# A statically scheduled spectral and attention kernel: background matmul jobs cut into pieces, VectorE operations placed around GpSimd, new scheduler constants

## Chip, cores, metric

One core of one Trainium2 chip. The metric is device time in microseconds (us) of one execution. Before: 1383.79 us, median of 3 runs (1383.43 to 1384.35). Engines: PE is TensorE (PEld its weight loads), DVE is VectorE, ACT is ScalarE, POOL is GpSimd.

## The reference

Two pairs of layers over a sequence of 2048 rows of 512: an FFT filter with a residual, then attention with 32 query heads and one shared K and V of 16 channels (the code is abbreviated here).

```python
def _A_ref(x, w_r, w_i):                     # spectral filter
    X = rfft2(x.astype(float32)) * (w_r + 1j * w_i)
    return irfft2(X).astype(bfloat16)
def _B_ref(x, wq, wk, wv, wo):               # 32 heads of 16, one K and V
    q, k, v = heads(x @ wq), x @ wk, x @ wv
    p = softmax(einsum("bhqd,bkd->bhqk", q, k) * 16 ** -0.5)
    return merge(einsum("bhqk,bkd->bhqd", p, v)) @ wo
x = x + _A_ref(_layernorm(x), A_w_r, A_w_i)
x = x + _B_ref(_layernorm(x), B_wq, B_wk, B_wv, B_wo)
# ... and both once more
```

## The kernel before

The program is written by a list scheduler in Python. It keeps a clock for each engine, chooses the next instruction by it, and emits every engine's stream in that order. On the chip the streams run in order and meet at semaphores. The order is fixed, so an engine that is late makes the others wait.

Softmax tiles are shared out. ACT exponentiates pairs (`exp`); DVE makes single tiles by an affine map to the bits of a bfloat16 (`p1`), and POOL adds two constant offsets to those bits (`phase`). PE makes scores, 32-row matmuls, and the products with V ("pv"), 32-column matmuls. Everything else on PE is a *background job* of full 128x128 matmuls, put between scores and pv. Each of these three tile shapes is a *mode* of PE; background jobs are the *full* mode.

```python
class Plan:
    MM, ACT_EXP, DVE_P1, POOL_PH = 216.0, 905.0, 600.0, 1200.0     # (cut: more constants)
    WARM, FORCE, HOLD, GAP = 3500.0, 3150.0, 200.0, 3000.0         # (one line each in the kernel)
    def do_bg(self, start, k):                # a background job goes in whole
        eng = k.eng
        if eng == "PE":
            self.fill(start, "full")          # filler matmuls where PE was too idle
            # (cut)
        k.fn(k)
        k.end = self.t[eng] = start + k.dur
    def pe_next(self):
        # (cut: candidates for scores and pv)
        c += self.bg_next("PE")
        return self.least(c)

# a projection: four matmuls, 870 ns, one job
m = p.add("PE", 870.0, deps, lambda k, r=r: em.proj(at, t, r, k.slot, 0, 4), take="b", prio=-2, gap=p.GAP)

def phase(self, t, p, n, eng):
    if eng == "POOL":
        self.nc.gpsimd.int64_add(t[p][:, 0:n].bitcast(U64), t[0][:, 0:n].bitcast(U64), DELTA[p] * FOUR)
    # (cut)
def mul(self, at, b):                         # normalise: two inputs in SBUF, on DVE
    # (cut)
    self.nc.vector.tensor_tensor(out=on.rearrange("p a h d -> p h a d"), in0=raw[:, :, :, 0:16],
                                 in1=rc.unsqueeze(3).to_broadcast([P, 2, 16, 16]), op=ALU.mult)
```

The FFT butterflies (`radix4`) are DVE operations with two SBUF inputs too. Some of those for layer 2 run within layer 1's attention. `fill` adds matmuls on zeros when the last 3.4 us of PE's plan hold too little work.

The softmax here doesn't subtract the row's maximum and nothing guards it: scores larger than these inputs give would overflow.

## Time and profile before

| stretch (us from the start) | what | us |
|---|---|---|
| 0 to 125.3 | FFT; then K and V are built, with first scores | 125.3 |
| 125.3 to 702.0 | attention 1, from DVE's first tile to its last | 576.7 |
| 702.0 to 812.9 | FFT and build of layer 2 | 110.9 |
| 812.9 to 1370.2 | attention 2 | 557.3 |
| 1370.2 to 1381.0 | last projections | 10.8 |

The borders are the first and last bit-trick tile of DVE in each layer. From the page of the kernel before: busy time by engine, two lines of the busy tenths (the span in 40 slices, each digit the busy share of one in tenths), and three groups of instructions (busy us, mean ns, idle before them and what ended it).

```profile
PE 1333.4 (97%) x13112; PEld 439.6 (32%) x13112; DVE 1309.3 (95%) x2345; ACT 1249.1 (90%) x1396; POOL 828.6 (60%) x805
...
DVE  6987999999999999999979879999999999999998
ACT  6488999999999999999954889999999999999996
...
L1085 ACT ACTIVATE e<-sa 128x1024 bf16<-128x1024 f32 x1251 | 1175.1, 1037 | 46.1 <-PE sa L1080 27.1
L1096 POOL INT64_ADD w<-w x795 | 826.2, 1051 | 541.9 <-DVE w L1092 494.0
L1092 DVE TENSOR_SCALAR w<-b 128x512 uint16<-128x512 f32 x1594 | 984.3, 681 | 15.6 <-PE b L1080 8.9
```

DVE and ACT are nearly full in attention and less so in two short stretches. A busy time includes the overlap with the next instruction: exponentials start every 904 ns and DVE tiles every 598 ns when nothing holds them up. The same by stretch (busy us of each engine, granted clock, DMA):

```profile
core 0: us, PE busy (x) PEld busy (x) DVE busy (x) ACT busy (x) POOL busy (x), PEclk, DMA share, GB/s
0.00:125.30 125.30, 119.04 (x884) 63.34 (x885) 99.94 (x263) 85.40 (x123) 2.35 (x10) 1.00 0.29 90
125.30:702.00 576.70, 561.37 (x5730) 161.99 (x5730) 566.12 (x948) 555.33 (x603) 411.46 (x394) 1.00 0.02 5
702.00:812.90 110.90, 105.82 (x810) 56.41 (x810) 89.46 (x223) 67.30 (x94) 1.04 (x1) 1.00 0.15 47
812.90:1370.20 557.30, 541.01 (x5645) 155.81 (x5645) 547.32 (x904) 540.68 (x580) 412.81 (x400) 1.00 0.01 4
```

L1120 is the multiply `mul`, L75 a butterfly step. The view of one line's instructions gives minimum, median and maximum in ns:

```profile
L1120 DVE TENSOR_TENSOR on<-raw,rc x32: 681/686/1539, 150.1 to 1373.6; 128x512 bf16<-128x512 f32 x32
...
L75 DVE TENSOR_TENSOR gx<-w x8: 281/286/1119, 17.3 to 720.6; 128x256 bf16<-128x256 bf16 x8
```

Same operation, same size, yet up to 858 ns longer. The timeline of DVE and POOL around the longest multiply (start us, length us) shows when:

```profile
1056.48 2.01 DVE L1092 TENSOR_SCALAR w<-b 128x512 uint16<-128x512 f32 x3
1058.41 1.54 DVE L1120 TENSOR_TENSOR on<-raw,rc 128x512 bf16<-128x512 f32 x1
1059.87 2.47 DVE L1092 TENSOR_SCALAR w<-b 128x512 uint16<-128x512 f32 x4
...
1057.35 2.06 POOL L1096 INT64_ADD w<-w  x2 [0.52 <-DVE w L1092]
```

POOL's second add begins at 1058.36, 45 ns before the multiply, and ends at 1059.40; the multiply ends half a microsecond later.

### The profile page before, as it was taken

The page shows a single profiled execution, that of the slowest core. Times are in us where ns is not written, and L with a number is a line of the kernel's source. Part 1 is how long each engine was busy: PE and PEld are TensorE (multiplying, and loading weights), DVE is VectorE, ACT ScalarE, POOL GpSimd, SP SyncE. Part 2 cuts the span into 40 slices and gives each one's busy share as a digit, 9 for nine tenths or more (in the row PEclk, how much of TensorE's full clock was granted, in tenths as well). Part 3 has the DMA queues.
Part 4 walks back from the last instruction along what each step waited for, and adds up shares of the span by engine and source line. Part 5 has one row for each costly group of instructions (what it writes and reads, how often), then busy time and mean ns, then how long its engine had stood idle before and what let it go on. Part 6 is the DMA issues. An engine that isn't in the chain of part 4 may idle for free. (4 is left out here: it accounts for less than half of the span.)

```text
span 1381.0 us, 32833 instructions
## 1 busy us (share of the span) xinstructions
PE 1333.4 (97%) x13112; PEld 439.6 (32%) x13112; DVE 1309.3 (95%) x2345; ACT 1249.1 (90%) x1396; POOL 828.6 (60%) x805
## 2 busy tenths in 40 slices
PE   9999999999999999999999999999999999999998
PEld 5643222222223222322246432222222222222222
DVE  6987999999999999999979879999999999999998
ACT  6488999999999999999954889999999999999996
POOL 0001777767775677667730027777777767776775
PEclk9999999999999999999999999999999999999999
DMA  9100000000000000000051000000000000000000
GB/s 284 39 1 1 2 2 2 2 1 2 1 1 2 1 1 2 1 1 1 2 161 39 1 1 2 1 2 13 6 1 2 5 13 2 2 2 17 2 2 16
DMA packets 20937, 22.08 MB, mean 16 GB/s; under 512 B 2096, under 2 KB 19504, under 8 KB 20784
## 3 DMA queue, kind: packets, MB, share of 16 engines
q1 hardware_dynamic: 20496, 19.44, 4.5%
q8 instruction: 102, 1.67, 0.5%
q10 hardware_dynamic: 288, 0.56, 0.1%
q14 instruction: 51, 0.42, 0.1%
HBM read 17.89 MB, written 2.10 MB: 14 GB/s over the span
## 5 line engine op out<-in xcount | busy, mean ns | idle before, releaser
L1085 ACT ACTIVATE e<-sa 128x1024 bf16<-128x1024 f32 x1251 | 1175.1, 1037 | 46.1 <-PE sa L1080 27.1
L1096 POOL INT64_ADD w<-w x795 | 826.2, 1051 | 541.9 <-DVE w L1092 494.0
L1092 DVE TENSOR_SCALAR w<-b 128x512 uint16<-128x512 f32 x1594 | 984.3, 681 | 15.6 <-PE b L1080 8.9
L1102 PE MATMUL b<-w,vs 128*32 128x512 bf16 x4782 | 532.9, 385 | 2.0 <-DVE w L1098 1.3
L1102 PE MATMUL b<-e,vs 128*32 128x512 bf16 x2502 | 434.4, 385 | 1.6 <-ACT e L1085 1.0
L1080 PE MATMUL sa<-w,KB 32*128 32x512 bf16 x1258 | 250.6, 381 | 13.8 <-ACT e L1085 11.0
L1102 PEld LDWEIGHTS <-vs 128*32 128x32 bf16 x7284 | 151.5, 94 | 349.4 <-issue 326.2
L1080 PE MATMUL sa<-w,KA 32*128 32x512 bf16 x1244 | 248.8, 382 | 10.6 <-ACT e L1085 8.0
L1080 PE MATMUL b<-w,KA 32*128 32x512 bf16 x804 | 245.7, 382 | 0.4
L1080 PE MATMUL b<-w,KB 32*128 32x512 bf16 x790 | 241.5, 382 | 2.9 <-DVE w L1092 2.6
L1080 PEld LDWEIGHTS <-KB 32*128 32x128 bf16 x2048 | 82.1, 91 | 234.8 <-issue 229.7
L1080 PEld LDWEIGHTS <-KA 32*128 32x128 bf16 x2048 | 80.4, 91 | 228.2 <-issue 224.2
L1011 DVE TENSOR_TENSOR x_sb<-b,x_sb 128x512 bf16<-128x512 f32 x64 | 42.6, 679 | 11.9 <-PE b L1006 6.0
L1109 DVE STREAM_TRANSPOSE raw<-b 128x512 f32<-128x512 f32 x64 | 45.3, 708 | 1.7 <-PE b L1102 1.6
L846 DVE BATCH_NORM_STATS2 st<-x_sb 128x6 f32<-128x512 bf16 x64 | 43.5, 679 | 3.4 <-DMA x_sb<-in_A_x_dram 3.1
L1064 PE MATMUL b<-gx,wq 128*128 128x512 bf16 x128 | 33.0, 380 | 1.3 <-DVE w L1092 1.0
L1133 PE MATMUL b<-WO,w 128*128 128x512 bf16 x128 | 32.2, 380 | 0.7 <-DVE w L1092 0.2
L987 PE MATMUL b<-it,xd 128*128 128x256 bf16 x256 | 30.0, 273 | 2.5 <-DVE xd L57 2.5
L1006 PE MATMUL b<-tab_PS,w 128*128 128x512 bf16 x128 | 31.4, 381 | 0.0
L896 PE MATMUL b<-tab_PH,e 128*128 128x512 bf16 x128 | 30.8, 380 | 0.6 <-DVE w L1092 0.2
L833 PE MATMUL b<-zero 128*128 128x512 bf16 x76 | 24.1, 411 | 5.3 <-DVE w L1092 2.4
L993 ACT CAST e<-b 128x512 bf16<-128x512 f32 x32 | 18.0, 583 | 12.0 <-PE b L987 12.0
(85 smaller groups left out, 605.2 us busy)
## 6 DMA issues: line engine op xcount, KB each, us to landing
it<-const_IT SPq DMA_DIRECT2D x8, 640.0 KB, 6.4
w<-const_FT SPq DMA_DIRECT2D x8, 512.0 KB, 7.4
x_sb<-in_A_x_dram SPq DMA_DIRECT2D x4, 512.0 KB, 6.8
w<-in_A_w_r_dram SPq DMA_DIRECT2D x8, 256.0 KB, 7.0
w<-in_A_w_i_dram SPq DMA_DIRECT2D x8, 256.0 KB, 7.6
out_dram<-x_sb SPq DMA_DIRECT2D x16, 128.0 KB, 1.8
tab_PH<-const_PH ACTq DMA_DIRECT2D x1, 512.0 KB, 5.0
tab_PS<-const_PS SPq DMA_DIRECT2D x1, 512.0 KB, 7.8
```

Of the source, the lines that this page charges most:

```text
L846: self.nc.vector.bn_stats(st, self.x[:, x[1], x[0], :])
L896: self.nc.tensor.matmul(self.ps(slot), lhsT=xt[:, i, cc, :], rhs=self.PH[:, cc, :], start=(cc == 0), stop=(cc == NC - 1), skip_group_check ...
L1006: self.nc.tensor.matmul(self.ps(slot), lhsT=L.UT[t][:, b, r, 128 * i:128 * i + 128], rhs=self.PS[:, 2 * i + b, :], start=(i == 0 and b == ...
L1011: self.nc.vector.tensor_tensor(out=x, in0=self.ps(slot), in1=x, op=ALU.add)
L1064: self.nc.tensor.matmul(self.ps(slot), lhsT=self.wq[:, c, g * 128:(g + 1) * 128], rhs=self.xTc(at, qb, c), start=(c == 0), stop=(c == NC - ...
L1080: self.nc.tensor.matmul(o, lhsT=KX[rs, kc * P:(kc + 1) * P], rhs=at.QT[qb][rs, g, :], start=True, stop=True, skip_group_check=True)
L1085: self.nc.scalar.activation(out=e, in_=self.ps(slot), func=ACT.Exp, scale=SCALE)
L1092: self.nc.vector.tensor_scalar(out=t[0][:, j], in0=self.ps(slot), scalar1=P1_SCALE, scalar2=P1_BIAS, op0=ALU.mult, op1=ALU.add)
L1096: self.nc.gpsimd.int64_add(t[p][:, 0:n].bitcast(U64), t[0][:, 0:n].bitcast(U64), DELTA[p] * FOUR)
L1102: self.nc.tensor.matmul(self.ps(slot)[32 * h:32 * h + 32, :], lhsT=V[:, kc, :], rhs=rhs, start=first, stop=last, skip_group_check=True)
L1109: self.nc.vector.transpose(out=at.raw[(qb, g)][:, par].rearrange("p a b -> p (a b)"), in_=self.ps(slot))
L1133: self.nc.tensor.matmul(self.ps(slot), lhsT=at.OT[t][:, g, r * P:(r + 1) * P], rhs=self.WO[:, g, :], start=(g == 0), stop=(g == 3), skip_g ...
```

## The change

The intent is to stop a four-matmul background job from holding up a score that is due, and to keep two-input DVE operations out of POOL's way. Arithmetic stays the same. The core of the diff (the same `parts=` is given to nearly every kind of background job, whose emitters now emit one piece):

```diff
-    WARM = 3500.0
-    FORCE = 3150.0
+    WARM = 3600.0
+    FORCE = 3350.0
-    HOLD = 200.0
+    HOLD = 250.0
-    GAP = 3000.0
+    GAP = 0.0
+    SLIP = 250.0
+    PATIENT = 1500.0
+    URGE = 300.0
+    STARVED = 6000.0
@@ bg_next
+            if k.port:
+                busy = self.t["POOL"]
+                for e in self.pool:
+                    if e[0] < max(start, busy) + k.dur:
+                        busy = max(busy, e[0]) + self.POOL_PH
+                start = max(start, busy - 160.0)
             # (cut)
+            if k.step:
+                prio = -4
+            elif eng == "PE" and self.t[eng] - max(ready, k.born) > self.STARVED:
+                prio = -3
@@ do_bg
+            n = min(steps, k.parts - k.step)
+            # (cut) emits n pieces; the job ends with its last piece
@@ pe_next
-        c += self.bg_next("PE")
+        for b in self.bg_next("PE"):
+            k, n = b[3], 99
+            late = T - max(b[4], k.born)
+            if kinds and c[0][0] <= b[0] + k.dur + self.PE_SW:
+                room = max(limit, c[0][0]) + self.SLIP - b[0] - self.PE_SW
+                fit = int(room / (k.dur / k.parts)) if room > 0 else 0
+                left = k.parts - k.step
+                if fit < left:
+                    need = min(left, 2) if late < self.PATIENT else 1
+                    n = max(fit, 1) if late > self.STARVED else fit if fit >= need else 0
+            if n:
+                c.append((b[0] - (self.URGE if kinds and late > self.PATIENT else 0.0),) + b[1:5] + (n,))
@@ jobs
-            m = p.add("PE", 870.0, deps, lambda k, r=r: em.proj(at, t, r, k.slot, 0, 4), take="b", prio=-2, gap=p.GAP)
+            m = p.add("PE", 870.0, deps, lambda k, s, r=r: em.proj(at, t, r, k.slot, s, s + 1), parts=4, take="b", prio=-2, gap=p.GAP)
-        mu = p.add("DVE", 660.0, [rc], lambda k: em.mul(self, b), lazy=tail)
+        mu = p.add("DVE", 660.0, [rc], lambda k: em.mul(self, b), lazy=tail, port=True)
```

The `port` rule also covers the butterflies. It lets such an operation start only when POOL, by the scheduler's clock, should be done.

## The prediction

> **What bounds the kernel now.** Attention fills two stretches (125 to 701 and 813 to 1381 us of the span); FFT and projections fill the rest. In attention three engines are nearly full at once (windows view, 1000 to 1100 us: PE 97.0, DVE 99.1, ACT 98.3 us of 100). Softmax tiles are shared between ACT (1251 exponentials, 904 ns start to start) and DVE (1594 bit-trick tiles, 598 ns). PE has little slack: slots in one mode start 216 to 226 ns apart, slots across a mode change 320 to 325 ns, so a change costs about 100 ns; 1056 changes and 1902 slots fill some 520 of the last 568 us. The Trainium skill, "TensorEngine Tiling (Array Packing)", Key Properties, says that a mode switch drains the array; this trace agrees, with those 100 ns.
>
> Start-to-start time beyond the usual adds up in the attention stretches to 74 us on ACT, 38 of them behind a full-mode PE job (projection, QT, front), and to 53 us on DVE, 17 behind such a job: four matmuls hold PE for 870 ns while a score tile is due.
>
> **What the change does.** It rewrites the static scheduler; arithmetic is unchanged. By the instruction orders:
> - Background PE jobs may be cut into single matmuls. Full-mode runs of four matmuls between scores fall from 98 to 14, all full-mode runs rise from 146 to 224, mode changes from 2318 to 2427: 109 x 100 ns = 11 us more of PE.
> - 9 exponentials more (9 x 904 ns = 8.1 us of ACT), 18 DVE tiles fewer (18 x 598 ns = 10.8 us), 9 POOL adds fewer. While K and V are built, each layer runs 49 exponentials instead of 44, in ACT's idle time, and filler there drops from 31 to 8 matmuls.
> - DVE operations with two SBUF inputs are placed where POOL should be idle. The Trainium skill, "SBUF — State Buffer", SBUF: two separate sides, says that such an operation and a GpSimd operation lock each other out for a whole instruction. The trace agrees: 10 of 32 normalising multiplies took over 830 ns, up to 1539 instead of 681 (3.7 us together), and butterflies in the first attention lost about 5 us.
>
> **On the critical path.** Attention shortens only if ACT and DVE both need less time. DVE: -10.8 for tiles, -6 for locks (most of 8): about -17 us, nearly all on the path, and a few us of its 17 behind full-mode jobs. ACT, outside the build stretches, keeps its exponentials (583 and 579, before 584 and 579), so it must lose about 9 us of idle per layer, half of its 19 behind full-mode jobs, which finer cutting makes plausible. FFT stretches (0 to 74, 701 to 762 us) keep their order and time. The 11 us of mode changes eat PE slack of some 45 us per layer, and may give back a little in waits for scores.
>
> **Prediction.** 1365 us, -1.4%; 8 in 10 between 1353 and 1379 us. Faster by over 2%: 0.15; within 2%: 0.84; slower by over 2%: 0.01.
>
> **What would show it.** DVE busy down by 15 to 20 us, with 1576 tiles; longest multiply below 900 ns; ACT's excess behind full-mode jobs in attention down from 38 to about 20 us; FFT stretches equally long; both attention stretches shorter by 8 to 10 us each.
>
> **What would make it wrong.** If the added mode changes make PE the last to be ready, idle time only moves from "behind a full job" to "waiting for scores": 1375 us or more. If POOL drifts from the scheduler's clock, locks stay: +6 us. If projections without their 3 us spacing pile up, ACT stalls in bursts. If DVE idle falls as much as its busy time, it goes below 1356 us.

## More of the kernel before

Adding up what two-input DVE operations took beyond their usual time, where that is over 150 ns, gives 9.9 us in 19 operations, all in attention. I call this sum the *lock time*.

## The result, and the profile after

1371.79 us, median of 12 runs (1370.70 to 1379.54); before, in all 15 runs up to then, 1383.76 us. The ratio of the fast runs is 0.9913, 95% interval 0.9899 to 0.9927. A ratio is the mean time of one kernel's fast runs over that of the other's of the same rounds, so it is not quite the ratio of the medians. The one run at 1379.54 had a mean granted clock of 0.991, the others 0.997 to 1.000.

The page after, the lines that answer to those of before:

```profile
PE 1328.9 (97%) x13077; PEld 426.7 (31%) x13077; DVE 1292.9 (94%) x2326; ACT 1258.3 (92%) x1405; POOL 809.3 (59%) x796
...
DVE  7887999999999999999979879999999999999998
ACT  6488999999999999999953989999999999999996
...
L1128 ACT ACTIVATE e<-sa 128x1024 bf16<-128x1024 f32 x1260 | 1184.9, 1042 | 27.3 <-PE sa L1123 18.4
L1139 POOL INT64_ADD w<-w x786 | 806.9, 1038 | 549.9 <-DVE w L1135 497.4
L1135 DVE TENSOR_SCALAR w<-b 128x512 uint16<-128x512 f32 x1576 | 977.2, 682 | 22.1 <-PE b L1123 11.0
```

DVE is 16.4 us less busy, ACT 9.2 us more. By stretch, cut at the same events:

```profile
0.00:127.80 127.80, 122.57 (x885) 63.24 (x886) 100.86 (x263) 89.84 (x128) 2.35 (x10) 1.00 0.28 88
127.80:695.00 567.20, 553.20 (x5717) 157.22 (x5717) 555.21 (x940) 554.75 (x602) 400.35 (x390) 1.00 0.02 5
695.00:807.90 112.90, 108.97 (x814) 56.15 (x810) 90.38 (x223) 71.72 (x99) 1.04 (x1) 1.00 0.14 43
807.90:1358.70 550.80, 538.54 (x5622) 148.04 (x5622) 539.95 (x894) 541.92 (x580) 404.49 (x394) 1.00 0.02 5
```

Attention 1 lost 9.5 us and attention 2 6.5 us; the two stretches with a build in them grew by 2.5 and 2.0 us. The multiply (now L1163) and the butterfly, in the view of one line:

```profile
L1163 DVE TENSOR_TENSOR on<-raw,rc x32: 653/682/692, 160.3 to 1362.5; 128x512 bf16<-128x512 f32 x32
...
L75 DVE TENSOR_TENSOR gx<-w x8: 284/286/294, 17.8 to 713.6; 128x256 bf16<-128x256 bf16 x8
```

No operation is held up any more: the lock time is 0. So the account for DVE is:

| term | us |
|---|---|
| 18 tiles fewer, 598 ns each | -10.8 |
| lock time | -9.9 |
| other start-to-start excess in the two attentions: 51.6 - 9.9 = 41.7 before, 46.8 after | +5.1 |
| the two stretches with a build | +4.5 |
| sum | -11.1 |

The profiled span went from 1381.0 to 1369.9 us, -11.1 us (0.4 us more in the tail are within the rounding of such a sum). "Start-to-start excess" is the time between the starts of consecutive instructions on an engine, minus the 20th percentile for that kind of instruction, summed. A recount from the two traces, where it is positive, gives 52.4 - 9.9 = 42.5 before and 46.9 after, so the third term is known to about 1 us. The same recount for ACT gives 74.1 us of excess in the two attentions before and 59.0 after: 8.1 us less in attention 1 and 7.0 in attention 2, about as much as these stretches lost.

### The profile page after: what moved, and what is told of

Its sections match the earlier page's. It is cut to its first block, busy times and chain, and to the rows that moved or that the text cites. A ratio compares the mean times of both kernels' runs of the same rounds, so it can differ in the third digit from the quotient of the medians.

```text
span 1369.9 us, 32779 instructions
## 1 busy us (share of the span) xinstructions
PE 1328.9 (97%) x13077; PEld 426.7 (31%) x13077; DVE 1292.9 (94%) x2326; ACT 1258.3 (92%) x1405; POOL 809.3 (59%) x796
## 5 line engine op out<-in xcount | busy, mean ns | idle before, releaser
L1139 POOL INT64_ADD w<-w x786 | 806.9, 1038 | 549.9 <-DVE w L1135 497.4
L1145 PE MATMUL b<-w,vs 128*32 128x512 bf16 x4728 | 526.3, 385 | 3.3 <-DVE w L1141 2.1
L1123 PE MATMUL sa<-w,KB 32*128 32x512 bf16 x1268 | 262.5, 382 | 9.4 <-ACT e L1128 6.6
L1123 PE MATMUL b<-w,KB 32*128 32x512 bf16 x780 | 251.9, 382 | 0.6 <-DVE w L1135 0.3
L1145 PEld LDWEIGHTS <-vs 128*32 128x32 bf16 x7248 | 145.0, 94 | 326.2 <-issue 304.5
L1058 DVE TENSOR_TENSOR x_sb<-b,x_sb 128x512 bf16<-128x512 f32 x64 | 42.5, 678 | 6.5 <-PE b L1053 4.9
L1107 PE MATMUL b<-gx,wq 128*128 128x512 bf16 x128 | 38.3, 384 | 0.2 <-DVE w L1135 0.2
L882 PE MATMUL b<-zero 128*128 128x512 bf16 x89 | 28.3, 409 | 4.1 <-ACT gx L1068 1.2
```

Source lines behind the costliest of these rows:

```text
L1058: self.nc.vector.tensor_tensor(out=x, in0=self.ps(slot), in1=x, op=ALU.add)
L1107: self.nc.tensor.matmul(self.ps(slot), lhsT=self.wq[:, c, g * 128:(g + 1) * 128], rhs=self.xTc(at, qb, c), start=(c == 0), stop=(c == NC - ...
L1123: self.nc.tensor.matmul(o, lhsT=KX[rs, kc * P:(kc + 1) * P], rhs=at.QT[qb][rs, g, :], start=True, stop=True, skip_group_check=True)
L1145: self.nc.tensor.matmul(self.ps(slot)[32 * h:32 * h + 32, :], lhsT=V[:, kc, :], rhs=rhs, start=first, stop=last, skip_group_check=True)
```

## The experiments

An account of one engine adds up by construction and does not say what caused what. Two theories stood: **cutting** makes the gain, or **locks** do. A third came with the first runs: locks also cost clock. All times below are medians; before is 1383.7 to 1384.0 us.

A first group takes parts of the change away, or one part alone. In a second group the *order is kept* and only the lock is taken out. A change of a scheduling rule re-deals all later instructions; the second group is free of that.

### b_nolock: before, in its own order, without locks

```diff
-            self.nc.gpsimd.int64_add(t[p][:, 0:n].bitcast(U64), t[0][:, 0:n].bitcast(U64), DELTA[p] * FOUR)
+            self.nc.gpsimd.memset(t[p][:, 0:n].bitcast(F32), 1.0)
```

> The kernel before in its own instruction order, with one edit: the POOL add of a softmax phase becomes a memset of the same bytes, which reads no SBUF (the result is wrong on purpose). If the skill's lock rule holds, no multiply takes over 700 ns any more and DVE is some 8 us less busy or held up. Theory 'locks were on the path': 1375 to 1378 us. Rival 'DVE time freed by locks is swallowed by waits for ACT and PE in a fixed order': 1381 to 1384 us.

Measured: 1373.96 us, ratio 0.9940 (0.9919 to 0.9961), result wrong. Its line view of the multiply:

```profile
L1120 DVE TENSOR_TENSOR on<-raw,rc x32: 678/680/693, 150.7 to 1364.9; 128x512 bf16<-128x512 f32 x32
```

(One of its six runs took 1384.26 us, at a mean clock of 0.990; the others 1373.3 to 1374.0 at 0.999 to 1.000.) The gain is 9.7 us for 9.9 us of lock time, a little more than the lock theory expected. So a held-up DVE held up the others in this fixed order: without locks ACT's excess in the attentions falls too, from 74.1 to 65.9 us (the recount above).

### b_lock_nodep: the control

The memset also frees POOL from waiting for DVE's tile. So the add is kept, but reads a constant table.

```diff
-            self.nc.gpsimd.int64_add(t[p][:, 0:n].bitcast(U64), t[0][:, 0:n].bitcast(U64), DELTA[p] * FOUR)
+            self.nc.gpsimd.int64_add(t[p][:, 0:n].bitcast(U64), self.PH[:, 0:n].bitcast(U64), DELTA[p] * FOUR)
```

> Control for b_nolock: the kernel before in its own order, the POOL add kept, but reading a constant SBUF table in place of the tile that DVE just wrote (wrong result on purpose). It has the lock and not the data dependency. If the lock cost the 10 us that b_nolock won: no gain, 1382 to 1385 us, long multiplies still there. Rival 'b_nolock won because POOL no longer waits for DVE's tile': 1373 to 1376 us.

Measured: 1397.03 us, ratio 1.0083, clock 0.995 to 0.996. The range was missed, on the side that speaks for the lock. The multiply's median is now 958 ns:

```profile
L1120 DVE TENSOR_TENSOR on<-raw,rc x32: 680/958/1534, 156.6 to 1388.2; 128x512 bf16<-128x512 f32 x32
```

POOL, without its wait, ran ahead into the FFT stretches, where DVE is full of two-input butterflies. Measured against the usual lengths in the kernel before, the lock time is 26.9 us, of which 11.0 us are outside attention. Those stretches grew by 6.6 and 4.9 us. In the attentions the lock time rose from 9.9 to 15.8 us, and their length from 576.7 and 557.3 to 579.9 and 557.9 us. So, if a lock costs its own length, the missing wait gave about 2 us and not the 9.7 of b_nolock, and 17.0 us more of lock made the profiled span 14.6 us longer. How much of this is the lock itself is not told apart: the clock of this profile is at half for 13.65 us, and in both FFT stretches that begins within a hole in PE's stream, or 1.1 us after it (3.62 and 3.40 us long), in which PE waits for a butterfly.

### a_memset: the other control

The edit of b_nolock on the changed kernel, whose lock time is already 0.

> The changed kernel in its own order with the memset of b_nolock (wrong result on purpose). Its trace has no locks left, so if the lock is what the memset removes, nothing changes: 1370 to 1373 us. If the memset helps in another way: 1362 to 1366 us.

Measured: 1370.18 us, ratio 0.9894. The edit does little else than remove locks: the medians are 1.6 us apart, and the ranges (1368.56 to 1375.96 here) overlap.

### a_cut_only: cutting alone

```diff
-            if k.port:
+            if False:
-    WARM = 3600.0
-    FORCE = 3350.0
+    WARM = 3500.0
+    FORCE = 3150.0
-    HOLD = 250.0
+    HOLD = 200.0
-    GAP = 0.0
+    GAP = 3000.0
```

> The changed kernel with the port rule off and the old GAP, WARM, FORCE and HOLD, so that cutting of background PE jobs (with its urgency rules) is what is left. Theory 'cutting gives the gain': 1373 to 1378 us, with some 8 us of locks still in the trace. Rival 'locks and the new constants give it': 1381 us or more.

Measured: 1382.80 us, ratio 0.9991 (0.9975 to 1.0007): no gain, as the rival expected. But the runs spread from 1379.37 to 1386.01 us with their mean clocks:

| clock | 0.996 | 0.996 | 0.993 | 0.991 | 0.988 | 0.988 |
|---|---|---|---|---|---|---|
| us | 1379.37 | 1379.40 | 1381.83 | 1383.77 | 1385.93 | 1386.01 |

0.8 us for each thousandth. The windows of its profile around one drop:

```profile
322.00:335.00 13.00, 11.41 (x120) 3.26 (x118) 13.00 (x22) 11.57 (x13) 7.55 (x8) 1.00 0.00 1
335.00:349.00 14.00, 14.00 (x86) 2.33 (x84) 10.65 (x18) 10.13 (x10) 6.61 (x7) 0.51 0.00 1
349.00:362.00 13.00, 12.97 (x139) 3.86 (x139) 12.22 (x21) 12.50 (x14) 8.74 (x9) 1.00 0.01 2
```

For 14 us the clock is 0.51, and DVE and ACT are busy for 10.65 and 10.13 us only. What came just before, in the timelines of DVE and of PE:

```profile
331.39 0.26 DVE L74 TENSOR_TENSOR gx<-w 128x256 bf16<-128x256 bf16 x1
331.59 1.15 DVE L75 TENSOR_TENSOR gx<-w 128x256 bf16<-128x256 bf16 x1
332.66 1.12 DVE L76 TENSOR_TENSOR gx<-w 128x256 bf16<-128x256 bf16 x1
333.70 0.28 DVE L77 TENSOR_TENSOR gx<-w 128x256 bf16<-128x256 bf16 x1
...
332.65 0.42 PE L1145 MATMUL b<-w,vs 128*32 128x512 bf16 x4
334.64 0.38 PE L1145 MATMUL b<-w,vs 128*32 128x512 bf16 x1 [1.57 <-DVE w L1135]
```

Two locked butterflies of 1.15 and 1.12 us in place of 0.29, then a hole of 1.57 us in PE's stream in which it waits for a DVE tile, then half clock. The other drop of this profile, at 492 us, also follows locked L75 and L76 steps, at 487.5 and 488.6 us. The Trainium skill, "TensorE: Matmul & The Clock Gate", Part 1, says that a monitor of PE's activity halves the clock, in windows of about 3.4 us. The trace agrees on the length: the two drops last 13.65 and 10.24 us, four and three times 3.41. A hole of this length is no sure sign of a drop: in the profile of the kernel before, PE has one of 1.29 us at 742.5 us, in an FFT stretch, and the clock stays whole.

### a_cut_only_nolock: the same order without locks

The edit of b_nolock on a_cut_only.

> The order of a_cut_only with the memset in place of the add (wrong result on purpose). Theory 'lock stalls open holes in PE's stream, and the clock then drops to half for some us': clock back to 0.998 or more, 1366 to 1373 us, 10 us or more below a_cut_only. Rival 'the dips come from the cut order and the smaller filler themselves': clock again 0.988 to 0.996, 1374 to 1379 us.

Measured: 1366.03 us, ratio 0.9866 (0.9842 to 0.9890), clock 1.000 in five of six runs. The same window of its profile:

```profile
335.00:349.00 14.00, 13.95 (x141) 4.03 (x142) 13.71 (x23) 13.97 (x16) 8.08 (x10) 1.00 0.01 2
```

16.8 us for a lock time of 10.8 us: the locks cost their own length and the clock on top. (By the 0.8 us per thousandth above, the lost clock, 0.992 in the median run, is some 6.6 us of this; an estimate.) Without locks one run in six still lost clock (0.995, 1371.13 us), with them all six did. Locks alone do not bring the drops, though: the kernel before has 9.9 us of them, and its clock was 0.998 or more in 29 of the 33 runs. Nor are locks the only cause: the profiles of a_memset, a_no_port_nolock, a_old_filler and a_hold245 each have a drop of 3.41 us at 129 to 130 us with no lock before it. What brings those stays open. Against b_nolock, which has the old order and no locks either, cutting with its urgency rules is worth 1374.0 - 1366.0 = 8.0 us, in an order dealt anew (a_hold245 below shows how much that alone can move). Both theories hold, and they are not independent: with locks in, the gain of cutting is lost.

### a_no_port and a_no_port_nolock

The first is the changed kernel with `if k.port:` made `if False:`; the second adds the memset.

> The changed kernel with the port rule off alone. If locks cost what they hold up, 8 us come back: 1380 us or more. If most of it is swallowed by other waits, 1374 to 1379 us; the order also changes elsewhere (7 DVE tiles more), which alone may cost some us.

Measured: 1387.30 us, ratio 1.0033; clocks 0.993 to 0.998; lock time 11.2 us. Slower than before.

> The order of a_no_port with the memset in place of the POOL add (wrong result on purpose). Theory 'locks and the clock dips they cause': 12 to 17 us below a_no_port, 1371 to 1376 us, clock 0.998 or more. Rival 'the order of a_no_port is bad by itself': 1380 us or more.

Measured: 1377.11 us, ratio 0.9958; 10.2 us below a_no_port, clock 0.991 to 1.000. The first run is where the lock theory put it, the second just outside its range: the locks are two thirds of the 15.5 us that a_no_port lost against the change, and some 5 us are its order. The pairs together:

| order of | lock time | with the add | with the memset | difference |
|---|---|---|---|---|
| before | 9.9 | 1383.7 | 1374.0 | -9.7 |
| a_no_port | 11.2 | 1387.3 | 1377.1 | -10.2 |
| a_cut_only | 10.8 | 1382.8 | 1366.0 | -16.8 |
| the change | 0.0 | 1371.8 | 1370.2 | -1.6 |

### a_whole: everything but cutting

```diff
-        for b in self.bg_next("PE"):
-            # (cut: the whole loop that counts pieces)
+        c += self.bg_next("PE")
```

> The changed kernel with cutting and the urgency rules off (a background PE job is put in whole, as before), port rule and new constants kept. Theory 'cutting gives the gain': slower than before, 1388 to 1396 us, ACT's excess behind full-mode jobs in attention back to about 38 us. Rival 'locks and constants give it': 1370 to 1378 us.

Measured: 1386.29 us, ratio 1.0022 (1.0010 to 1.0034), no locks, clock 0.997 to 1.000. The time falls between the two ranges, 1.7 us short of the cutting theory's. ACT's excess behind full-mode jobs in attention is 20.9 + 22.6 = 43.5 us (before 37.7, after 18.7; counting what has a full-mode matmul in the 1.5 us before its end gives 44.0, 39.1 and 19.1). So without cutting the other parts gave no gain: the 14.5 us to the change are over three times what a_hold245 moved. And these parts have a price: this kernel has no locks and the old kind of jobs, as b_nolock has, and is 12 us slower (some 1.6 of them by the memset). It avoids locks by putting operations later; together with the new constants, and in this order, that costs about what the locks did. Which of the three it is was not tested.

One rival stays open here. A new order also deals the tiles anew: DVE gets 1572 in a_old_filler (1371.8 us), 1576 in the change (1371.8), 1580 in a_hold245 (1375.9), 1584 in a_build_whole (1377.2) and 1604 here (1386.3). In these five orders with the port rule the time goes up with DVE's tiles, from end to end about 0.5 us for each, and a tile takes 598 ns. So cutting may gain mostly by letting the scheduler give DVE fewer tiles. b_nolock, with 1594 tiles and 1374.0 us, shows that this is not all.

### a_old_filler

WARM 3500 and FORCE 3150 in the changed kernel.

> The changed kernel with the old filler thresholds (WARM 3500, FORCE 3150: 80 filler calls in place of 112), port rule and cutting kept. If filler keeps the clock up: dips as in a_cut_only, mean clock below 0.997, 1376 us or more. If the absence of locks keeps it up: clock 0.998 or more, 1371 to 1375 us.

Measured: 1371.82 us, ratio 0.9907, clock 0.992 to 1.000: the same as the change. The filler thresholds are not what keeps the clock up; without locks the smaller filler does as well (its run of 1378.5 us at 0.992 has its like in the change, 1379.54 at 0.991).

### a_build_whole

```diff
             k, n = b[3], 99
+            if self.at is not None and not self.at.dve_on:
+                c.append(b)
+                continue
```

> The changed kernel, but while K and V are being built background PE jobs go in whole (42 exponentials before the first DVE tile, in place of 50). Theory 'interleaved scores hold up the build by 2 us': stretch from the end of the first attention's DVE tiles to the second's first one 109 to 111 us, after 112.9; first DVE tile at 124 to 126 us, after 127.8. The total is not to be read: the later order is re-dealt (10 us more is possible).

Measured: 1377.18 us, ratio 0.9959. DVE's first tile comes at 124.0 us and the second such stretch is 109.0 us long, as expected:

```profile
0.00:124.00 124.00, 117.14 (x854) 62.92 (x868) 100.00 (x264) 83.38 (x121) 2.35 (x10) 1.00 0.29 90
124.00:699.60 575.60, 560.86 (x5725) 158.70 (x5754) 558.21 (x939) 560.91 (x608) 400.70 (x390) 1.00 0.02 5
699.60:808.60 109.00, 103.94 (x780) 55.94 (x792) 89.53 (x223) 65.86 (x93) 1.04 (x1) 1.00 0.14 44
```

So the interleaved scores do stretch the build, by 3.8 to 3.9 us each here. Whether they pay for it in attention is not told apart: attention 1 is 8.4 us longer, in an order dealt anew.

### a_hold245

HOLD 245 in place of 250 in the changed kernel.

> The changed kernel with HOLD 245 in place of 250, which should mean nothing, yet re-deals the whole order (1580 DVE tiles in place of 1576). Theory 'a good part of the gain is that this setting was picked': slower by 4 to 10 us, 1376 to 1382 us, with no locks and a clock of 0.998 or more. Rival 'the mechanism gives the gain whatever the setting': 1370 to 1373 us.

Measured: 1375.90 us, ratio 0.9940 (0.9927 to 0.9953), lock time 0.3 us, clock 0.998 to 1.000. The low edge of the range was missed by 0.1 us. A step in one constant that should mean nothing costs 4.1 us, a third of the gain. So some of the 12 us may be the luck of how this order fell.

### a_pool_mul: a candidate that failed

On the changed kernel, with HOLD 150, WARM 3550, FORCE 3250, SLIP 200 and PATIENT 3000 as well:

```diff
-        mu = p.add("DVE", 660.0, [rc], lambda k: em.mul(self, b), lazy=tail, port=True)
+        mu = p.add("POOL", 1300.0, [rc], lambda k: em.mul(self, b))
-        self.nc.vector.tensor_tensor(out=on.rearrange("p a h d -> p h a d"), in0=raw[:, :, :, 0:16],
+        self.nc.gpsimd.tensor_tensor(out=on.rearrange("p a h d -> p h a d"), in0=raw[:, :, :, 0:16],
```

> A correct candidate: the changed kernel with the 32 normalising multiplies on POOL, where they cannot be locked out by POOL's own adds and leave DVE 22 us of work less, butterflies still under the port rule, and settings picked anew (HOLD 150, WARM 3550, FORCE 3250, SLIP 200, PATIENT 3000). If DVE work and locks are what count: 1360 to 1367 us. If POOL's multiply is slow (over 1.6 us) or locks out butterflies: 1370 us or more.

Measured: 1856.28 us, ratio 1.3409, correct. The multiply itself takes 1047 ns, which the candidate allowed for. From the view of its line, and from the groups on POOL:

```profile
L1163 POOLq MODIFY_POOL_CONFIG  x64: 6/11/13, 145.1 to 1846.7; - x64
L1163 POOL TENSOR_TENSOR on<-raw,rc x32: 1044/1047/1048, 151.8 to 1853.6; 128x512 bf16<-128x512 f32 x32
```

```profile
L1139 POOL INT64_ADD w<-w x790 | 811.0, 1038 | 766.7 <-DVE w L1135 553.7 <-issue 180.5 <-PE b L1123 21.9
L1163 POOL TENSOR_TENSOR on<-raw,rc 128x512 bf16<-128x512 f32 x32 | 33.5, 1047 | 229.1 <-issue 229.1
```

Two configuration loads stand before each multiply, and two more before the next add; the kernel before has two in all. POOL is idle for 229.1 / 32 = 7.2 us before a multiply and 180.5 / 31 = 5.8 us before the add after it, 410 us in all. The Trainium skill, "GPSIMD Engine Reference", 2.1 Instruction dispatch, gives about 6 us for the first call to freshly loaded code, without a visible instruction; 5.8 and 7.2 us fit that, though no run took the loads away. The mean clock fell to 0.829 as well. No version that is correct beat the change.

## Why the prediction was right, and where its sizes were off

- **Direction and range held**: 1371.8 us lies within 1353 to 1379, and within 2% of before. The centre, 1365, asked for 19 us; the chip gave 12.
- **Cutting: right.** ACT's excess behind full-mode jobs in attention went from 38 to 18.7 us, as forecast. ACT "must lose about 9 us of idle per layer", said the prediction; by the recount it lost 8.1 and 7.0 us of its whole excess. So of the 19 us won behind full-mode jobs about 4 came back in other waits, as the prediction feared, on a small scale. In orders without locks cutting is worth 8.0 us.
- **Locks: right, under-sized.** "DVE: ... -6 for locks (most of 8)". The lock time was 9.9 us (3.7 in multiplies as stated, 6.1 in butterflies, not "about 5"), and taking it out of the old order gave 9.7 us. The longest multiply fell to 692 ns, below the 900 forecast. POOL's drift did not bring locks back.
- **DVE busy time: right.** 16.4 us less, 1576 tiles. (Busy time counts the overlap of neighbours once, so it is not the sum of the terms above.)
- **The step that was mis-sized, on DVE's side: "nearly all on the path, and a few us of its 17 behind full-mode jobs".** DVE's work fell by 20.7 us (tiles and locks), more than forecast. But DVE's wait behind full-mode jobs stayed at 16 us, and its other excess in attention rose by 4 to 5 us in sum. Attention 2 became shorter by 6.5 us, not by 8 to 10.
- **A term that was missing: the build.** The prediction counted the five added exponentials per build as use of idle time. The FFT before it kept its time as forecast (first exponential 74.3 us from the start, and 59.9 us after attention 1; 75.0 and 60.1 in the change). The two stretches grew by 2.5 and 2.0 us; a_build_whole shows that interleaving does this.
- **A price that was missing: the port rule and the constants, perhaps.** Without locks and with the memset in both, the order of a_cut_only takes 1366.0 us and the order of the change 1370.2 us. The 4.2 us are the price of the added waits and constants, or of how the order happened to fall: a_hold245 shows that 4 us can come from nothing else. Which, stays open.
- **The feared rival, mode changes of PE, is not it.** a_cut_only_nolock has 2451 of them, more than the change (2427), and is the fastest; a_whole has 2326 and is among the slowest (counted in the traces).
- **Not foreseen at all**: the granted clock. With the locks in, a_cut_only loses clock in every run, and nearly its whole gain. That the change avoids this is luck as far as the prediction goes.

## What to carry to other kernels

In streams that run in a fixed order and wait for each other, a stall on one nearly full engine can be a stall of all: here 9.9 us of stalls cost 9.7. Price it in full, and look whether it opens a hole in PE's stream with a drop of the clock after it. To find what a stall costs, keep the order and take the stall away, even with a wrong result; an edit of the scheduling rule deals a new order, and a step of 5 in one constant moved this kernel by 4 us. Two changes that look separate can need each other: cutting was worth 8 us without the locks and 1 us with them, in the one cut order that was tried both ways.

## What the Trainium skill lacked or had wrong

- "TensorEngine Tiling (Array Packing)", Key Properties: gives no time for a mode switch. Here slots across a switch start 320 to 325 ns apart, in one mode 216 to 226: about 100 ns.
- "TensorE: Matmul & The Clock Gate", the closing table of advice: warns of gaps over about 3 us. Here a hole of 1.57 us, in 13 us with PE busy for 11.41, came just before a drop to half clock that lasted 13.65 us. The page's section on a second failure mode speaks of micro-idles without giving their length.
- "SBUF — State Buffer", SBUF: two separate sides: says that the lock blocks the loser, not what it costs a kernel whose engines wait for each other. Here 9.9 us of lock time cost 9.7 us, and 10.8 us cost 16.8 where the clock fell too.
- "GPSIMD Engine Reference", 2.1 Instruction dispatch: speaks of the first call to freshly loaded code; it does not say that two operations in turn can cost this each time. Here an integer add and a multiply in turn left POOL idle for some 12.8 us per multiply, with two configuration loads at each turn.
